# The last pair of token chunks takes w4 in seven block products for eight, and gives its output transposed

## The chip, the cores and the metric

One core of one Trainium2 chip runs the whole program. The metric is the device time of one execution in microseconds; of several executions the median is taken.

## The reference

Two layers, and each adds two parts to a residual stream `x` of 2048 tokens by 512 channels: a Fourier mixing by matrix products, and an MLP block. The second half of the MLP block, which the change is about, is a gelu between two matrices of 512 x 1376 and 1376 x 512.

```python
x1 = x + hs
h2 = _gelu(_layernorm(x1, axis=-1) @ w3) @ w4
return x1 + h2
...
x = A_x
x = x + _A_ref(_layernorm(x, axis=-1), A_dft_seq_re, A_dft_seq_im, A_dft_hid_re, A_dft_hid_im)
x = x + _B_ref(_layernorm(x, axis=-1), B_w1, B_w2, B_w3, B_w4)
x = x + _A_ref(_layernorm(x, axis=-1), A_dft_seq_re, A_dft_seq_im, A_dft_hid_re, A_dft_hid_im)
x = x + _B_ref(_layernorm(x, axis=-1), B_w1, B_w2, B_w3, B_w4)
```

## The kernel before

All numbers are fp32. A product of two fp32 blocks is made of three matmuls (`mm3`): each operand is split into a high part (a cast to fp32r on ScalarE, "ACT") and a low part (a subtraction on VectorE, "DVE"), and high x high, high x low and low x high are added up in PSUM. So every operand tile costs one ACT and one DVE instruction beside the matmuls that use it, and every block product of 128 x 128 by 128 x 512 costs three matmuls on TensorE ("PE").

The Fourier part streams the big matrices from HBM: a piece of 512 KB lands in one of four `raw` buffers (`issue_dma`, line 205), is split or summed into one of four `ring` slots by `stage_one` and `stage_two` (lines 220 to 241), and is used by the matmuls. Each layer goes over four chunks `c` of 512 tokens; for a chunk an x phase (`x_phase`) is followed by a y phase (`y_phase`). The x phase calls `hook(i)` at 16 steps, and what stands in the hook is put into the instruction streams there.

The MLP part (`by_pairs`) takes the tokens as two pairs of chunks, `c1` and `c2`. The hidden width is padded to 11 tiles of 128 channels (`NF`). A pair begins with the odd tile (w3e), and then goes over five steps `p`, of two hidden tiles each. In each step w3 is taken by seven products for eight (`prod`, a Strassen scheme with the sums of the inputs in `blk` and of the outputs in `u`, `v`, `x`, `y`), 42 matmuls of 512 columns. Its w4 products are plain ones: `w4_part` adds one hidden tile into four PSUM banks of 128 tokens by 512 channels, with the hidden tile as the stationary operand and w4 as the moving one: 12 matmuls for each tile and chunk. Those of `c1` stand between the steps, those of `c2` after them, and the results are added to `x` (`drain`) and stored.

There is one list of instructions for each engine, in the order in which the code is written; no scheduler moves them. All loads and stores are issued by SyncE ("SP") in that order too, so a load that waits for its buffer holds back every later one. Of the transfers in flight at most eight are allowed: each also waits for the one issued eight places earlier.

Of the kernel before, what the change touches and what calls it, by code (L numbers as in the profile page):

```python
# [8 lines left out]
F32 = mybir.dt.float32  # L9
F32R = mybir.dt.float32r  # L10
AF = mybir.ActivationFunctionType
ALU = mybir.AluOpType

P = 128
S, D, F = 2048, 512, 1376
# [4 lines left out]
CH = 512  # L20
NC = S // CH
TC = CH // P
KD = D // P
DH = D // 2
NF = -(-F // P)
B = 32
NB = P // B
LAG = 2
# [14 lines left out]
def spectral_mlp_kernel(ctx: ExitStack, tc: tile.TileContext, x, ws, hs, w1, w2, w34, out):  # L43
    nc = tc.nc
# [3 lines left out]
    dram = ctx.enter_context(tc.tile_pool(name="dram", bufs=1, space=bass.MemoryType.DRAM))  # L48
    ctx.enter_context(tc.manual_schedule())

    tmp = const.tile([P, 6, D], F32, name="tmp")
# [8 lines left out]

    w3d = [dram.tile([P, 2, 7, 2 * P], F32, name=f"w3d{i}") for i in range(NF // 2)]
    w3e = dram.tile([P, 2, CH], F32, name="w3e")
    w4d = [dram.tile([P, 2, CH], F32, name=f"w4d{i}") for i in range(NF)]


# [4 lines left out]
    AX, AY = 3 * 2 * DH, 4 * 2 * DH  # L70
    W12, XS = 2 * ZW, 2 * ZW + 8 * 2 * CH
    H3 = XS + NT * D
    SPARE = H3 + (LAG + 1) * 2 * CH
    RR = SPARE + 2 * D
    RNG = RR + 2 * KD * 2 * CH
    base = -(-nc.sbuf_base // 32) * 32
    EXT = RNG + RING * 4 * CH
    RAWS = EXT + 6 * D
    STG = RAWS + RAW * 2 * CH
    nc.alloc_sbuf_tensor("arena", [P, STG + 2 * CH], F32)  # L80

    def at(name, word, *shape, dtype=F32R):
        return nc.alloc_sbuf_tensor_at(name, [P, *shape], dtype, offset=base + 4 * word).ap()

    def both(name, word, *shape):
        return at(name, word, *shape), at(name + "f", word, *shape, dtype=F32)
# [7 lines left out]
    xs = [at(f"xs{i}", XS + i * 2 * D, 2, D, dtype=F32) for i in range(NP)]  # L94
# [8 lines left out]
    blk, blkf = {}, {}  # L103
# [4 lines left out]
    w3b, w3bf = zip(*(both(f"w3b{i}", RNG + 8 * CH + i * 28 * P, 2, 7, 2 * P) for i in range(2)))  # L108
    h4 = [at(f"h4{i}", RR + 8 * CH + i * 2 * CH, 2, CH) for i in range(4)]
# [7 lines left out]
    rest = [at(f"rest{i}", RAWS + i * D, D, dtype=F32) for i in range(8)]  # L117

    def xt(j):
        return xs[j // 2][:, j % 2]  # L120

    PA, PB, PC, PD = ([psum.tile([P, CH], F32, name=f"ps{i}{j}") for j in range(2)] for i in "abcd")
    acc4 = PC + PB
    mm4 = PD + PA
# [30 lines left out]
    for layer in range(LAYERS):  # L155
        for c in range(NC):
# [5 lines left out]
            for k in range(NP):  # L162
# [4 lines left out]
                p = piece(ws[c, k][:, 2:4])  # L167
# [26 lines left out]
    def rows(sb, d, j, n, load):  # L194
        v = d[j * P : (j + n) * P, :].rearrange("(t p) d -> p t d", p=P)
        nc.sync.dma_start(*((sb, v) if load else (v, sb)))
# [77 lines left out]
        return slots.pop(i)  # L274


    def mm3(o, lh, ll, rh, rl, first, last):
        nc.tensor.matmul(o, lh, rh, start=first, stop=False)  # L278
        nc.tensor.matmul(o, lh, rl, start=False, stop=False)  # L279
        nc.tensor.matmul(o, ll, rh, start=False, stop=last)  # L280

    def stats(srcs):

# [140 lines left out]
    def low(tf):  # L424
        nc.vector.tensor_tensor(tf[0][:, :, 1], tf[1][:, :, 1], tf[0][:, :, 0].bitcast(F32), op=ALU.subtract)
# [37 lines left out]
    def add(o, a, b, op=ALU.add):  # L463
        nc.vector.tensor_tensor(o, a, b, op=op)  # L464
# [123 lines left out]
    def turn_one(t, q, u):  # L588
        v = t.rearrange("p d (a q j) -> p d a q j", a=NB, q=TC)[:, :, :, q]
        nc.vector.transpose(v, blocks_of(u))  # L590

    def turn_out(t, to=None):

        if to is None:
            count["turn"] += 1
            to = zd[count["turn"] % 2]
        z = to.rearrange("(e i) t -> i e t", i=B)
        for b in range(NB):
            v = t[b * B : (b + 1) * B].rearrange("i d (a t) -> i (d a) t", a=NB)
            nc.sync.dma_start(z[:, :, b * P : (b + 1) * P], v)  # L600
# [35 lines left out]
    def split(dst, g, copy=nc.vector.tensor_copy):  # L636
        copy(dst[:, 0], g)  # L637
        split_low(dst, g)
# [74 lines left out]

        add(*(blkf[i][:, :, 1] for i in (o, a, b)), ALU.subtract)

    def prod(o, w, u, b):
        for d in range(2):
            v = slice(d * P, (d + 1) * P)
            mm3(o, w[:, 0, u, v], w[:, 1, u, v], blk[b][:, d, 0], blk[b][:, d, 1], d == 0, d == 1)

    def last_of(layer):
        return layer == LAYERS - 1
# [4 lines left out]
    def by_pairs(layer, zs, xin, dst):  # L727
# [78 lines left out]
        def w4_load():  # L806
            n = seq["n"]
            if n == n_pairs * len(order) or layer == 0 and n >= len(order) and n - used["n"] > 3:
                return
            src, i = order[n % len(order)], w4_slot(n)  # L810
            nc.sync.dma_start(w4r[i].bitcast(F32), w3e if src is None else w4d[src])
            seq["n"] += 1

        def w4_use():
            used["n"] += 1
            return w4r[w4_slot(used["n"] - 1)]
# [141 lines left out]
        def drain(c, acc):  # L958
            for q in range(TC):
                nc.vector.tensor_tensor(xt(c * TC + q), acc[q], xt(c * TC + q), op=ALU.add)  # L960
# [7 lines left out]
        def one():  # L968
            if bg:
                bg.pop(0)()  # L970
# [41 lines left out]

        for pair in range(n_pairs):
            c1, c2 = 2 * pair, 2 * pair + 1
            kept, next_too = bool(layer or pair), pair == n_pairs - 1 and not last_of(layer)
            hcs = [hc[:, f] for f in range(NF)]
            if next_too:
# [1 line left out]
                bg += early  # L1019
            if pair:  # L1020
                bg.insert(0, lows("t4"))
            sets = [rest[4:8], [tmp[:, i] for i in range(4)] if layer and pair else rest[4:8]]
            bk, acc1 = (acc4, mm4) if pair == 0 else (mm4, acc4)
            acc2 = [bk[(1 + i) % 4] for i in range(4)]
            if pair == 0:
# [132 lines left out]
                    rows(xs[j // 2], dst, j, 2, False)  # L1158
            split_later(2)
            split_later(3)  # L1160
            last = layer and pair == n_pairs - 1
            for k in range(NF - 2 if last else NF):
                w4_part(acc2, fs[k], h4[(2 + k) % 4])
                w4_load()
                if k:
                    split_later(k + 3)
                one()
                after_part(k + 2)
            if last:
                ss = [w4_use(), w4_use()]  # L1170
                for q in range(TC):
                    v = slice(q * P, (q + 1) * P)
                    for k, s in zip((NF - 2, NF - 1), ss):
                        h = h4[(2 + k) % 4]
                        mm3(acc2[q], h[:, 0, v], h[:, 1, v], s[:, 0], s[:, 1], False, k == NF - 1)
                    j = c2 * TC + q
                    nc.vector.tensor_tensor(xt(j), acc2[q], xt(j), op=ALU.add)
                    rows(xs[j // 2][:, j % 2 : j % 2 + 1], dst, j, 1, False)
            else:
                drain(c2, acc2)  # L1180
                for j in range(c2 * TC, c2 * TC + TC, 2):
                    rows(xs[j // 2], dst, j, 2, False)
                while bg:
                    one()


    w4_from = [(w34[NF - 1][:, 0], w3e)] + [(w34[f + LAG][:, 1], w4d[f]) for f in range(NF)]
# [2 lines left out]
    def w4_split(i):  # L1190
        for n in (i - 5, i - 4, i - 3):
            if 0 <= n <= NF:
                w, wf = w4_in[n % 4]
                if n == i - 5:
                    nc.vector.tensor_tensor(w[:, 1], wf[:, 1], w[:, 0].bitcast(F32), op=ALU.subtract)
                    nc.sync.dma_start(w4_from[n][1], w.bitcast(F32))
                elif n == i - 4:
                    nc.scalar.copy(w[:, 0], wf[:, 1])
                else:
                    nc.sync.dma_start(wf[:, 1], w4_from[n][0])  # L1200

    for layer in range(LAYERS):
        xin = x if layer == 0 else x2d
# [3 lines left out]
        for c in range(NC):  # L1207
# [82 lines left out]
            def hook(i):  # L1290
                k, odd = divmod(i, 2)
                if layer == 0 and c == 1:
                    if i == 1:
                        xp_sums(NP - 1)
                    if i == 2:
                        xp_highs(NP - 1, False)
                    if i == 3:
                        xp_lows(NP - 1, False)
                    w4_split(2 * NP + i)
                if c == 0:  # L1300
                    if layer:
                        for step, f in zip((0, 0, 1), (ay_sums, ay_highs, ay_lows)):
                            if i == step:
                                f(5)
                        for k, first, stages in (
                            (6, X6, xp_stages),
                            (7, X7, (xp_stats, xp_norm, ax_sums, ax_highs, ax_lows)),
                        ):
                            for step, f in zip((0, 1, 3, 4, 6), stages):
                                if i == first + step:  # L1310
                                    f(k)
                    return
                j = (c - 1) * TC
                if i == 4:
                    rows(X1, xin, j, 2, True)
                if i == 9:
                    rows(X1, x1d, j, 2, False)
                if i == 10:
                    rows(X1, xin, j + 2, 2, True)
                if c == NC - 1 and i in BACK:  # L1320
                    rows(xs[BACK[i] // 2], x1d, BACK[i], 2, True)
# [105 lines left out]
```

## Time and profile before

| | |
|---|---|
| times of 3 runs | 1442.24, 1442.72, 1443.43 us; median 1442.72 us |
| span of the profiled execution | 1440.5 us |
| PE busy | 1433.3 us, 6312 matmuls |
| DVE busy | 1127.9 us |
| ACT busy | 714.8 us |
| moved by DMA | 297.35 MB, mean 206 GB/s |

The span runs from the first to the last instruction of the profiled execution. A busy time is the time in which an engine has at least one instruction running; the matmuls overlap, so the busy time of PE is not the sum over them. For the profiled execution only the span is listed; its own time as the three runs are timed is not, so the median of the runs stands for it, 2.2 us above the span.

### The profile page before, as it was taken

What the parts mean: (1) busy time and instruction counts of PE and PEld (TensorE: products, weight loads), DVE (VectorE), ACT (ScalarE), POOL (GpSimd) and SP (SyncE); (2) the same over time, 40 slices, a digit from 0 to 9 for tenths busy, and PEclk for the clock granted to TensorE, in tenths of its full rate; (3) what the DMA queues carried; (4) which work ended last, traced back from release to release, by engine and by line L of the source; (5) the groups of instructions that cost most, each with busy time, mean ns of one, the idle gap of its engine ahead of it and who ended that gap; (6) DMA issues with size and microseconds to landing.
All of it is one profiled execution on the core that took longest, in us unless ns stands there. A gap on an engine that the chain in (4) does not pass through costs nothing.

```text
span 1440.5 us, 17253 instructions
## 1 busy us (share of the span) xinstructions
PE 1433.3 (99%) x6312; PEld 1181.6 (82%) x6312; DVE 1127.9 (78%) x1559; ACT 714.8 (50%) x954; POOL 82.2 (6%) x111
## 2 busy tenths in 40 slices
PE   9999999999999999999999999999999999999998
PEld 7888888888888888888888888888888888888887
DVE  7986997987969787666799979889798787656442
ACT  6663454455565644444555544545455574433231
POOL 2100000000002000000000000000000010000000
PEclk9999999999999999999999999999999999999999
DMA  7866655657655857944645565565666466578434
GB/s 258 268 205 204 205 185 197 203 179 258 206 175 130 289 199 239 364 159 154 239 142 189 190 199 196 168 228 173 231 216 225 141 178 252 199 246 322 161 127 158
DMA packets 117796, 297.35 MB, mean 206 GB/s; under 512 B 8784, under 2 KB 41552, under 8 KB 115152
## 3 DMA queue, kind: packets, MB, share of 16 engines
q1 hardware_dynamic: 117712, 296.26, 61.3%
q8 instruction: 49, 0.80, 0.2%
q14 instruction: 35, 0.29, 0.1%
HBM read 249.30 MB, written 46.92 MB: 206 GB/s over the span
## 4 chain that ended last, share of the span: by engine, by line
PE 95%; DVE 2%; ACT 1%; issue 1%; POOL 0%; DMA 0%; DVEq 0%; ACTq 0%; POOLq 0%
PE psd L278 10%; PE psd L280 10%; PE psd L279 10%; PE psa L278 8%; PE psa L280 8%; PE psa L279 8%; PE psc L280 7%; PE psc L279 7%; PE psc L278 7%; PE psb L278 7%; PE psb L279 7%; PE psb L280 7%; DVE ring L241 0%; DVE xs L960 0%; DVE ay L391 0%
## 5 line engine op out<-in xcount | busy, mean ns | idle before, releaser
L223 ACT CAST ring<-raw 128x1024 fp32r<-128x1024 f32 x127 | 132.9, 1052 | 88.3 <-PE psd L280 40.0
L241 DVE TENSOR_TENSOR ring<-raw,ring 128x1024 fp32r<-128x1024 f32 (+1 forms) x128 | 154.8, 1212 | 21.6 <-ACT ring L223 20.9
L279 PE MATMUL psd<-ring,rr 128*128 128x512 f32 x208 | 81.0, 389 | 0.0
L278 PE MATMUL psd<-ring,rr 128*128 128x512 f32 x208 | 81.0, 389 | 0.0
L280 PE MATMUL psd<-ring,rr 128*128 128x512 f32 x208 | 81.0, 389 | 0.0
L631 ACT ACTIVATE tmp<-rest 128x512 f32<-128x512 f32 x36 | 22.8, 632 | 95.7 <-DVE rest L464 95.4
L318 POOL TENSOR_TENSOR rs<-ve,mhalf 128x4 f32<-128x4 f32 x16 | 27.8, 1738 | 610.7 <-DVE nm L317 610.7
L230 ACT CAST ring<-ring0f 128x1024 fp32r<-128x1024 f32 x28 | 29.6, 1056 | 58.6 <-DVE ring0f L229 58.6
L634 DVE TENSOR_TENSOR h<-hc,h 128x512 fp32r<-128x512 f32 x41 | 27.9, 690 | 37.2 <-ACT h L637 37.2
L241 DVE TENSOR_TENSOR ring<-ring1f,ring 128x512 fp32r<-128x512 f32 (+1 forms) x56 | 53.3, 952 | 0.7 <-ACT ring L226 0.7
L297 POOL TENSOR_TENSOR rs<-ve,mhalf 128x2 f32<-128x2 f32 (+1 forms) x33 | 28.1, 853 | 413.5 <-DVE nb L296 413.5
L637 ACT CAST h<-hc 128x512 fp32r<-128x512 f32 x41 | 25.3, 620 | 51.1 <-PE psd L279 17.0
L279 PE MATMUL psb<-ring,ay 128*128 128x512 f32 x128 | 50.1, 391 | 0.0
L279 PE MATMUL psc<-ring,ay 128*128 128x512 f32 x128 | 49.9, 390 | 0.0
L280 PE MATMUL psc<-ring,ay 128*128 128x512 f32 x128 | 49.9, 390 | 0.0
L280 PE MATMUL psb<-ring,ay 128*128 128x512 f32 x128 | 49.8, 389 | 0.0
L278 PE MATMUL psc<-ring,ay 128*128 128x512 f32 x128 | 49.8, 389 | 0.0
L278 PE MATMUL psb<-ring,ay 128*128 128x512 f32 x128 | 49.8, 389 | 0.0
L279 PE MATMUL psa<-ring,ay 128*128 128x512 f32 x126 | 49.1, 390 | 0.0
L280 PE MATMUL psa<-ring,ay 128*128 128x512 f32 x126 | 49.1, 389 | 0.0
L278 PE MATMUL psa<-ring,ay 128*128 128x512 f32 x126 | 49.1, 389 | 0.0
L279 PE MATMUL psd<-ring,ay 128*128 128x512 f32 x126 | 49.1, 389 | 0.0
(440 smaller groups left out, 4419.2 us busy)
## 6 DMA issues: line engine op xcount, KB each, us to landing
raw<-in_ws SPq DMA_DIRECT2D x183, 512.0 KB, 5.0
w4r<-w4d SPq DMA_DIRECT2D x88, 512.0 KB, 4.2
raw<-in_hs SPq DMA_DIRECT2D x56, 512.0 KB, 3.7
w3b<-w3d SPq DMA_DIRECT2D x15, 1792.0 KB, 7.3
w3d<-w3b SPq DMA_DIRECT2D x5, 1792.0 KB, 6.9
x1d<-tmp SPq DMA_DIRECT2D x12, 512.0 KB, 6.3
xs<-x1d SPq DMA_DIRECT2D x12, 512.0 KB, 6.5
w4d<-w4in SPq DMA_DIRECT2D x11, 512.0 KB, 4.7
```

The source lines that it names most:

```text
L223: nc.scalar.copy(dest[:, a:b, 0], r[0][:, a:b])
L230: nc.scalar.copy(dest[:, :, 0], lo)
L241: nc.vector.tensor_tensor(lo[:, i], src[:, i], hi[:, i].bitcast(F32), op=ALU.subtract)
L278: nc.tensor.matmul(o, lh, rh, start=first, stop=False)
L279: nc.tensor.matmul(o, lh, rl, start=False, stop=False)
L280: nc.tensor.matmul(o, ll, rh, start=False, stop=last)
L297: nc.gpsimd.tensor_tensor(rs[:, :n], ve[:, :n], mhalf[:, 0, :n], op=ALU.pow)
L318: nc.gpsimd.tensor_tensor(rs, ve, mhalf[:, :, :2], op=ALU.pow)
L631: nc.scalar.activation(g_of, ps_of, AF.Gelu_apprx_tanh)
L634: nc.vector.tensor_tensor(dst[:, 1], g, dst[:, 0].bitcast(F32), op=ALU.subtract)
L637: copy(dst[:, 0], g)
```

## The change

The last pair of the second layer leaves the loop of `by_pairs` and gets a function of its own, `last_pair`. There the w3 steps run one behind the other, without w4 in between, and all 55 hidden tiles and sums are kept (`hs_`). Two hidden tiles by two chunks, and w4's two rows of tiles by two halves of 256 channels, then make a 2 x 2 block product, taken by the same seven products for eight: four of them in a first stretch over the five steps `k`, three in a second. w4 is the stationary operand now and the hidden tiles (512 tokens) are the moving one, so the output comes as channels by tokens. The odd tile (`h11`) is taken plainly. The residual is transposed on DVE (`turn_x`), written to HBM (`xtd`) and read back (`rt`). The upper half of the output is written transposed, and the host turns it back.

The sums of w4's blocks that the seven products need are made once, in the x phases of layer 0's chunks 2 and 3 and of layer 1's chunks 1, 2 and 3, one step `k` in each: a load at hook step 2, four sums on DVE and a cast on ACT at step 10, a subtraction on DVE and a store of 1 MB at step 11.

```diff
+    w4s = [dram.tile([P, 4, 2, 2 * P], F32, name=f"w4s{i}") for i in range(NF // 2)]
+    xtd = [dram.tile([D, CH], F32, name=f"xtd{i}") for i in range(2)]
...
         def w4_load():
             n = seq["n"]
             if n == n_pairs * len(order) or layer == 0 and n >= len(order) and n - used["n"] > 3:
+                return
+            if last_of(layer) and n > len(order):
                 return
...
+            if last_of(layer) and pair == n_pairs - 1:
+                last_pair(c1, c2, dst, w4_use)
+                continue
...
+    def last_pair(c1, c2, dst, w4_use):
...
+        w3c = [w3b[1], w3b[0], at("w3c", XS, 2, 7, 2 * P)]
+        w3c = [w3c[i] for i in (0, 1, 2, 0, 1)]
...
+        def load_1(k):
+            t = u1[k % 3].bitcast(F32)
+            for i in range(2):
+                nc.sync.dma_start(t[:, i], w4d[2 * k + i][:, :, : 2 * P])
+            nc.sync.dma_start(t[:, 2:4], w4s[k][:, 0:2])
...
+        def parts_of(of, k):
+            for f in (high_of, low_of):
+                for n in h_in_1 if of is hi_1 else h_in_2:
+                    f(of, k, n)
...
+        def product(o, w, hi, lo, first, last):
+            for i in range(2):
+                v = slice(i * P, (i + 1) * P)
+                mm3(o[i], w[:, 0, v], w[:, 1, v], hi, lo, first, last)
...
+        nc.sync.dma_start(w11.bitcast(F32), w4d[NF - 1])
+        load_1(0)
+        w3_bring(2)
+        for p in range(nk):
...
+            prod(b1, w, 4, "11")
+            act(u, b1)
+            prod(b6, w, 1, "t2")
+            add(v, u, b6)
+            then(0)
+            prod(b7, w, 2, "t3")
+            add(x, v, b7)
+            then(1)
+            prod(b5, w, 0, "t1")
+            add(y, x, b5)
+            gelu_to("22", y)
+            prod(b1, w, 5, "21", new=False)
+            gelu_to("11", b1)
+            then(2)
+            prod(b4, w, 6, "t4")
+            add(x, x, b4)
+            gelu_to("21", x)
+            then(3)
+            prod(b5, w, 3, "22", new=False)
+            add(v, v, b5)
+            gelu_to("t3", v)
+            if p < 2:
+                w3_bring(p + 3)
+            one()
+        load_1(1)
+        load_1(2)
+        parts_of(hi_1, 1)
+        t_sum(nk - 1, 0, 1, 2, 3)
...
+        for k in range(nk):
+            t = u1[k % 3]
+            for o, unit, n in ((p1, 0, "11"), (p6, 3, "t2"), (p5, 2, "t1"), (p2, 1, "21")):
+                if k == 0 and o is p2:
+                    product(p2, w11[:, :, : 2 * P], h11[0][:, 0], h11[0][:, 1], True, False)
+                product(o, t[:, unit], hi_1(k, n), hs_[k][n][0], k == 0 and o is not p2, k == nk - 1)
+            if k + 2 < nk:
+                parts_of(hi_1, k + 2)
+            else:
+                parts_of(hi_2, k + 2 - nk)
+            if k + 3 < nk:
+                load_1(k + 3)
+            load_2(k)
+            if k < 2:
+                nc.sync.dma_start(rt[k], xtd[k].rearrange("(d p) t -> p d t", p=P))
...
+        second(p4, 0, "t4", nk - 1, False)
+        for i in range(2):
+            add(v[:, i], v[:, i], p4[i])
+            store(v, c1, 1, i)
+        for i in range(2):
+            w = slice(i * P, (i + 1) * P)
+            t = u2[nk - 1][:, 2]
+            mm3(p3[i], t[:, 0, w], t[:, 1, w], hi_2(nk - 1, "22"), hs_[nk - 1]["22"][0], False, True)
+            add(x[:, i], x[:, i], p3[i])
+            store(x, c2, 0, i)
...
+        if i == 10:
+            a, b = (w4_raw[:, :, h * 2 * P : (h + 1) * 2 * P] for h in range(2))
+            s = w4_sumf[:, :, 1]
+            add(s[:, 0], b[:, 0], b[:, 1])
+            add(s[:, 1], s[:, 0], a[:, 0], ALU.subtract)
+            add(s[:, 2], a[:, 0], b[:, 0], ALU.subtract)
+            add(s[:, 3], a[:, 1], s[:, 1], ALU.subtract)
+            nc.scalar.copy(w4_sum[:, :, 0], s)
+        if i == 11:
+            nc.vector.tensor_tensor(
+                w4_sum[:, :, 1], w4_sumf[:, :, 1], w4_sum[:, :, 0].bitcast(F32), op=ALU.subtract
+            )
+            nc.sync.dma_start(w4s[k], w4_sum.bitcast(F32))
```

PE, in the last pair, between the w3 products of one step and of the next: before, the last matmuls of a plain w4 tile (stationary `h4`, moving `w4r`) are followed by w3's product with `t4` (`bt4`).

```order
L278 MATMUL psc1_241<-w4r2_211,h43_203 128x512
L279 MATMUL psc1_241<-w4r2_211,h43_203 128x512
L280 MATMUL psc1_241<-w4r2_211,h43_203 128x512
L278 MATMUL psb0_238<-w4r2_211,h43_203 128x512
L279 MATMUL psb0_238<-w4r2_211,h43_203 128x512
L280 MATMUL psb0_238<-w4r2_211,h43_203 128x512
L278 MATMUL psb1_239<-w4r2_211,h43_203 128x512
L279 MATMUL psb1_239<-w4r2_211,h43_203 128x512
L280 MATMUL psb1_239<-w4r2_211,h43_203 128x512
L278 MATMUL psa1_237<-bt4_194,w3b1_198 128x512
```

PE now, in the first stretch, at the change from step 0 to step 1: `hia` are the high parts of the hidden tiles, `hs` their low parts, `u1` the w4 blocks.

```order
L281 MATMUL psa0_243<-hs1_9387,u10_9481 128x512
L282 MATMUL psa0_243<-hia3_9459,u10_9481 128x512
L280 MATMUL psa1_244<-hia4_9460,u11_9482 128x512
L281 MATMUL psa1_244<-hs7_9399,u11_9482 128x512
L282 MATMUL psa1_244<-hia4_9460,u11_9482 128x512
L280 MATMUL psc0_247<-hia4_9460,u11_9482 128x512
L281 MATMUL psc0_247<-hs7_9399,u11_9482 128x512
L282 MATMUL psc0_247<-hia4_9460,u11_9482 128x512
```

The moving operand is still 512 columns wide, a hidden tile is used for two matmul groups instead of four, and over the whole program PE has 30 rows fewer.

DVE, in the x phase of layer 0's chunk 2, at hook steps 10 and 11 (before, then now; `ring` and `raw` are the stream's buffers, `ring1f` the sum of a slot):

```order
L241 TENSOR_TENSOR ring_170<-ring1f,ring_170 128x512
L241 TENSOR_TENSOR ring_172<-raw_176,ring_172 128x2x512
L241 TENSOR_TENSOR ring_174<-raw_177,ring_174 128x2x512
L225 TENSOR_TENSOR ring1f<-raw_178 128x512
L241 TENSOR_TENSOR ring_168<-raw_178,ring_168 128x2x512
```

```order
L243 TENSOR_TENSOR ring_177<-ring1f,ring_177 128x512
L243 TENSOR_TENSOR ring_179<-raw_183,ring_179 128x2x512
L466 TENSOR_TENSOR w4sumf<-w4raw 128x256
L466 TENSOR_TENSOR w4sumf<-w4sumf,w4raw 128x256
L466 TENSOR_TENSOR w4sumf<-w4raw 128x256
L466 TENSOR_TENSOR w4sumf<-w4raw,w4sumf 128x256
L243 TENSOR_TENSOR ring_181<-raw_184,ring_181 128x2x512
L1435 TENSOR_TENSOR w4sum<-w4sumf,w4sum 128x4x256
L227 TENSOR_TENSOR ring1f<-raw_185 128x512
```

Five instructions stand between those of the stream, and each place of the five has the same ones.

More of the change, by code (lines that the diff above doesn't have):

```diff
@@ L274, in stream, with mm3 @@
         return slots.pop(i)
[L277 to L280, printed above, removed]
+    def mm3(o, lh, ll, rh, rl, first, last, more=False):
+        nc.tensor.matmul(o, lh, rh, start=first, stop=False, skip_group_check=more)
+        nc.tensor.matmul(o, lh, rl, start=False, stop=False, skip_group_check=more)
+        nc.tensor.matmul(o, ll, rh, start=False, stop=last, skip_group_check=more)
     def stats(srcs):
@@ L714, in b_sum, with prod @@
         add(*(blkf[i][:, :, 1] for i in (o, a, b)), ALU.subtract)
-    def prod(o, w, u, b):
+    def prod(o, w, u, b, new=True):
         for d in range(2):
             v = slice(d * P, (d + 1) * P)
-            mm3(o, w[:, 0, u, v], w[:, 1, u, v], blk[b][:, d, 0], blk[b][:, d, 1], d == 0, d == 1)
+            mm3(o, w[:, 0, u, v], w[:, 1, u, v], blk[b][:, d, 0], blk[b][:, d, 1], new and d == 0, d == 1, not new)
     def last_of(layer):
@@ L1021, in by_pairs @@
                 bg.insert(0, lows("t4"))
-            sets = [rest[4:8], [tmp[:, i] for i in range(4)] if layer and pair else rest[4:8]]
+            sets = [rest[4:8], rest[4:8]]
             bk, acc1 = (acc4, mm4) if pair == 0 else (mm4, acc4)
@@ L1160, in by_pairs @@
             split_later(3)
-            last = layer and pair == n_pairs - 1
-            for k in range(NF - 2 if last else NF):
+            for k in range(NF):
                 w4_part(acc2, fs[k], h4[(2 + k) % 4])
@@ L1168, in by_pairs @@
                 after_part(k + 2)
[L1169 to L1178, printed above, removed]
-            else:
[L1180 to L1184, printed above, removed]
+            drain(c2, acc2)
@@ L1200, in w4_split, with w4_bring, w4_sums @@
                     nc.sync.dma_start(wf[:, 1], w4_from[n][0])
+    w4_raw = at("w4raw", STG, 2, CH, dtype=F32)
+    w4_sum, w4_sumf = both("w4sum", 5 * AY, 4, 2, 2 * P)
+    W4_AT = {(0, 2): 0, (0, 3): 1, (1, 1): 2, (1, 2): 3, (1, 3): 4}
+    def w4_bring(k):
+        nc.sync.dma_start(w4_raw, w34[2 * k + LAG : 2 * k + LAG + 2, :, 1].rearrange("f p w -> p f w"))
+    def w4_sums(k, i):
+        if i == 2:
+            w4_bring(k)
+        if i == 10:
[11 more added lines that the diff above has]
+            nc.sync.dma_start(w4s[k], w4_sum.bitcast(F32))
     for layer in range(LAYERS):
@@ L1312, in hook @@
                     return
+                if (layer, c) in W4_AT:
+                    w4_sums(W4_AT[layer, c], i)
                 j = (c - 1) * TC
@@ L1423 @@
     r = run_bass_kernel_spmd(nc, [arrays], core_ids=[0])
+    got, half = r.results[0]["out"], S // 2
     out = np.empty((S, D), a["A_x"].dtype)
-    out[at] = r.results[0]["out"]
+    out[at[:half]] = got[:half]
+    out[half:] = got[half:].reshape(D, half).T
     return out.reshape(_OUT)
```

122 lines of the change are left out of this document (added).

## The prediction

> **What bounds the kernel now.** The page comes first: how busy the engines are, and by what the chain that ended last is made.
>
> ```profile
> span 1440.5 us, 17253 instructions
> PE 1433.3 (99%) x6312; PEld 1181.6 (82%) x6312; DVE 1127.9 (78%) x1559; ACT 714.8 (50%) x954; POOL 82.2 (6%) x111
> PE 95%; DVE 2%; ACT 1%; issue 1%; POOL 0%; DMA 0%; DVEq 0%; ACTq 0%; POOLq 0%
> ```
>
> PE is busy for 99% of the span, and 95% of the chain is its matmuls. Next the waits of PE, over the whole program:
>
> ```profile
> PE psd L132 <- POOL mhalf L55: 1.4, 1, 1.4
> PE psc L279 <- DVE ring L241: 0.7, 1, 0.7
> PE psc L410 <- ACT rr L1242: 0.2, 1, 0.2
> ```
>
> PE waits 2.3 us in all, and never in the last pair. So whatever takes matmuls away shows in full, as long as the other engines and the loads keep up; and there is no wait left whose going could bring more. Last, what a matmul costs at its pace. These are the first and the last one of the last pair in the timeline (start, duration, engine, line):
>
> ```profile
> 1322.50 0.39 PE L278 MATMUL psd<-b,w4r 128*128 128x512 f32 x1
> ...
> 1435.15 0.39 PE L280 MATMUL psd<-w4r,h 128*128 128x512 f32 x1
> ```
>
> The code issues 498 matmuls here: 24 for w3e, 5 x 42 for w3, 22 x 12 for w4. From first to last there are 497 steps in 112.65 us, 0.2267 us each. The duration of 0.39 us overlaps the next ones, and is not the price.
>
> **The change part by part: matmuls.** All matmuls of the pair stay 512 columns wide. The plain w4 products were 2 chunks x 11 tiles x 12 = 264. Now the five steps take 7 products x 6 matmuls = 42 each, 210, and the odd tile 4 x 6 = 24: 234. That is 30 fewer, at 0.2267 us: **-6.80 us**. The roles of the operands are swapped, but both kinds of product lie in the same 112.65 us at one pace, so I take the pace as kept.
>
> The Trainium skill, page "TensorE: Matmul & The Clock Gate", section "Back-to-back issue gap", gives N / 2.4 + 2.5 ns, 215.8 ns for 512 columns; by it the sum would be -6.47 us. The trace has 226.7 ns, and the trace decides.
>
> **DVE and ACT in the last pair.** What the added instructions cost, from the groups of the lines view from 1270 us on (mean ns after the bar) and, for the transpose, from the view of its line (min/median/max):
>
> ```profile
> L464 DVE TENSOR_TENSOR rest<-rest,psd 128x512 f32<-128x512 f32 x11 | 7.6, 687 | 10.8 <-PE psd L280 10.8
> L634 DVE TENSOR_TENSOR h<-hc,h 128x512 fp32r<-128x512 f32 x22 | 15.0, 691 | 25.4 <-ACT h L637 25.4
> L464 DVE TENSOR_TENSOR bt2f<-b22f,bt1f 128x1024 f32<-128x1024 f32 x1 | 1.2, 1226 | 0.0
> L637 ACT CAST h<-hc 128x512 fp32r<-128x512 f32 x22 | 13.7, 621 | 33.9 <-PE psd L279 14.7 <-PE psc L279 7.7 <-PE psb L279 5.8
> L631 ACT ACTIVATE tmp<-rest 128x512 f32<-128x512 f32 x9 | 5.7, 632 | 32.7 <-DVE rest L464 32.7
> L590 DVE STREAM_TRANSPOSE scr<-rest x8: 668/708/712, 466.9 to 1180.3; 128x512 f32<-128x512 f32 x8
> ```
>
> A w3 step now lasts 42 x 0.2267 = 9.5 us on PE. DVE has 5 sums out of PSUM and from p = 1 on 4 sums of hidden tiles, 9 x 0.69 = 6.2 us; with two transposes 7.6 us; in the worst step, p = 3, three lows more: 8.3 us. ACT has 5 x 0.63 = 3.2 us, with four casts 5.6 us. It fits.
>
> The first stretch takes 24 x 0.2267 = 5.4 us a step, against 4 lows (2.8 us) and 4 casts (2.5 us). At its start the parts of step 1 follow the last sum (0.69), a gelu (0.63), a cast (0.62) and a low (0.69): the first pair is there after 2.6 us, and PE, with the odd tile's 6 matmuls in step 0, wants it after 30 x 0.2267 = 6.8 us. Those of step 2 stand behind the rest of them and four sums, and come until some 10.3 us; PE wants them at 12.2 us. In the second stretch a step is 4.1 us against three lows, 2.1 us. I cost all this at nothing; its cover is PE, and where it fails it costs the lateness itself.
>
> **The loads of the last pair.** w3's last three blocks now come within 43 us instead of being spread over twice that, and w4 comes in pieces. What the queue gives is read from the DMA view, for 1300 to 1330 us (runs of 2 KB and more) and 1240 to 1280 us (many runs of 512 bytes), and for 1322 to 1376 us, of which the second row is the landing time of one block of w3:
>
> ```profile
> DMA packets 2894, 10.01 MB, mean 334 GB/s; under 512 B 272, under 2 KB 272, under 8 KB 2759
> q1 hardware_dynamic: 2890, 9.97, 88.7%
> ...
> DMA packets 5283, 8.51 MB, mean 213 GB/s; under 512 B 240, under 2 KB 4336, under 8 KB 5026
> q1 hardware_dynamic: 5282, 8.49, 69.0%
> ...
> DMA packets 2053, 10.44 MB, mean 193 GB/s; under 512 B 195, under 2 KB 195, under 8 KB 1675
> w3b<-w3d SPq DMA_DIRECT2D x3, 1792.0 KB, 7.2
> ```
>
> The queue holds 334 GB/s over 30 us; with runs of 512 bytes 213 / 0.69 = 309 GB/s when it is busy. Now count from the pair's first matmul; I set the start of the flow at 5 us, since w4's first blocks wait for the second product of w3e (24 x 0.2267 = 5.4 us) and w3's block of p = 2 stands behind them on SP. Until PE wants that block at 5.4 + 2 x 9.5 = 24.4 us, 4.46 MB must come (output rows 1.05, `w11` 0.52, w4 1.05, w3 1.84): a rate of 4.46 / 19.4 = 230 GB/s. Until p = 4 at 43.6 us it is 9.2 MB (two blocks of w3 and a transposed residual more): 238 GB/s. In the first stretch the w4 blocks of k = 3 and k = 4, between them `u2` and `rt`, are 3.67 MB, free to be loaded from the end of step 0 on and wanted 16.3 us later: with 1.4 us of latency (my estimate, from the 2.0 us that 256 KB took to land, below, less their 0.7 at 334 GB/s) 246 GB/s. Runs of 1 KB, which these loads have, the trace does not show; they lie between the two rows, and I take the lower, 309. All three demands are below it, so this costs nothing; at 200 GB/s it would cost 11 us (rival C). Bounds: 0 to 11, the value 0 nearest to both rows.
>
> **The sums beside the x products.** At each of the five places DVE gets four sums of 256 columns. From 1226 ns for 1024 columns and 687 for 512 I estimate 0.42 us each, 1.7 us, and 1.22 us for the low; ACT one cast, about 1.05 us; SP two issues. DVE at the first place now, in the timeline and in the table of stages:
>
> ```profile
> 230.17 1.23 DVE L241 TENSOR_TENSOR ring<-raw,ring 128x1024 fp32r<-128x1024 f32 x1 [1.49 <-ACT ring L223]
> 233.13 0.69 DVE L225 TENSOR_TENSOR ring1f<-raw 128x512 f32<-128x512 f32 x1 [1.73 <-PE psa L280]
> ...
> 237.89 1.37 DVE L464 TENSOR_TENSOR tmp<-psd,tmp 128x512 f32<-128x512 f32 x2 [2.33 <-PE psd L280]
> ...
> 226.00:241.00 15.00, 15.00 (x68) 12.43 (x67) 8.56 (x10) 5.46 (x6) 0.03 (x1) 1.00 0.68 232
> ```
>
> DVE is idle for 15.00 - 8.56 = 6.4 us of these 15, in gaps that PE ends: it waits for PE to free a slot. 2.9 us go into that. On SP the store of the sums waits for the low, and behind it the next `raw` loads wait. They wait there anyway:
>
> ```profile
> SPq L205 <- DVE ring L241: 341.1, 121, 8.4
> ```
>
> The 1.5 MB of a place are some 5 us of the queue at 309 GB/s, in a phase that moves 232 GB/s. The ring holds up to four slots of 2.7 us (12 matmuls) each, so a few us of lateness do not reach PE. Zero, with bounds of 0 and 2 us over all five; a gain is excluded, since PE does not wait there.
>
> **The end.** Now four stores of 256 KB follow each other at 6 x 0.2267 = 1.36 us:
>
> ```profile
> 1434.22 0.69 DVE L1177 TENSOR_TENSOR xs<-psa,xs 128x512 f32<-128x512 f32 x1 [0.67 <-PE psa L280]
> 1435.58 0.69 DVE L1177 TENSOR_TENSOR xs<-psd,xs 128x512 f32<-128x512 f32 x1 [0.67 <-PE psd L280]
> ...
> out<-xs SPq DMA_DIRECT2D x4, 256.0 KB, 2.0
> ```
>
> In the changed kernel a result tile is finished every 3 matmuls, 0.68 us, and its sum takes 0.69: the last sum ends 0.05 us later than now after the last matmul. 256 KB each 0.69 us are 380 GB/s, at 334 each store takes 0.10 us more than its turn: about 0.3 us over the last four. Bounds: 0, and 1.6 at 213 GB/s. I take +0.3.
>
> **Sum.** -6.80 + 0.3 + 0 + 0 = -6.5 us: a span of 1434.0 for 1440.5. The three runs have their median at 1442.72, 2.2 us above the span; I take that as unchanged: **1436.2 us**.
>
> **The rivals.** *A, the forecast:* all cover holds, 1436.2; from 1435.2 (no cost at the end, and the 0.7 us by which runs of a kernel differ) to 1438. *B, a part is given back:* a late block of w3 or w4 in the last pair, 1 to 4 us, about 1438.7. For it: the demands of 230 to 246 GB/s are not far under 309, and a window of the pair moves only 193 GB/s now; against it: there SP waits for PE to free buffers, not the queue for bandwidth. *C, slower: the loads bound the last pair.* At 200 GB/s the block of p = 2 comes at 5 + 4.46 / 0.2 = 27.3 us, 2.9 late, that of p = 4 at 51 us, 7.4 late in all, and the w4 blocks of k = 4 3.5 us late: 11 us, so 1442.7 - 6.5 + 11 = 1447.2. It decides where lateness eats 6.5 us: 12.9 MB in 60 us, 215 GB/s. For it: the page's mean of 206 GB/s, and pieces of 1 KB and 512 bytes; against it: both rows above. *D, no change: the x phases pay.* If each place held up PE for 1.3 us, all 6.5 us would be gone, 1442.7. For it: SP stands still for the store, and the window moves 232 GB/s already; against it: the gaps on DVE and the ring's lead.
>
> What a long wait would do to the clock, the end of the trace hints at (window, PE and the other engines busy, granted clock third from the end):
>
> ```profile
> 1435.00:1440.50 5.50, 0.54 (x3) 0.12 (x1) 0.69 (x1) 0.00 (x0) 0.00 (x0) 0.92 0.28 105
> ```
>
> The Trainium skill, the same page, section "HAM oscillation — how this bites in real kernels", says that a gap of more than about 3.4 us halves the clock until PE has been busy again as long; in C that would add some 1.7 us for each wait of that length. The trace agrees as far as the clock falls to 0.92 in these idle us; C's price stands without it.
>
> **Numbers.** A 0.78, B 0.09, C 0.08, D 0.05. A measurement here tells 0.2% from no change, 2.9 us, so faster means under 1439.8: A and most of B, 0.86; same is D and the rest of B, 0.06; slower is C, 0.08. The range holds A and most of B: 1435.2 to 1439.5.
>
> **What would show it.** Right: 30 matmuls fewer on PE; the last pair 468 matmuls in about 106 us; PE's waits still some 2 us in all; the last store landing 2 to 2.3 us after its issue. Wrong: PE waiting for a DMA into `w3c`, `w3b` or `u1` (B, C), for `ring` in the five x phases (D), or for `hs` and `hia` (my count of DVE or ACT); or a pace other than 0.2267 us with the operands swapped.

## The result, and the profile after

| | before | after |
|---|---|---|
| median of 4 runs each | 1442.55 us (1442.24 to 1443.43) | 1435.47 us (1435.16 to 1435.71) |
| ratio | | 0.9951, 95% interval 0.9937 to 0.9965 |
| span of the profiled execution | 1440.5 us | 1433.3 us |

The change is faster by 7.1 us; 1436.2 had been forecast. The host's turning of the upper half of the output lies outside this time, and no run measures it. The page of the changed kernel, first the span, the busy times and what the chain is made of:

```profile
span 1433.3 us, 17344 instructions
PE 1426.0 (99%) x6282; PEld 1175.0 (82%) x6282; DVE 1168.3 (82%) x1629; ACT 728.3 (51%) x976; POOL 82.2 (6%) x111
PE 90%; DVE 6%; ACT 1%; DMA 1%; issue 1%; POOL 0%; SPq 0%; DVEq 0%; POOLq 0%; ACTq 0%
```

PE has 6282 matmuls for 6312, the 30 fewer of the forecast, and it is still busy for 99%. DVE has 70 instructions and 40.4 us more, ACT 22 and 13.5 us. The chain has 90% of PE for 95% before, but PE is not short of work for that: the waits say what it lacked (us in total, times, longest):

```profile
PE psd L134 <- POOL mhalf L55: 1.4, 1, 1.4
PE psc L281 <- DVE ring L243: 0.7, 1, 0.7
PE psb L412 <- ACT rr L1480: 0.6, 1, 0.6
PE psa L282 <- DVE rg L636: 0.6, 1, 0.6
PE psc L412 <- ACT rr L1480: 0.2, 1, 0.2
```

That is 3.5 us, all of it ahead of the last pair: from 1322 us to the end the view is empty. The first and the last matmul of the last pair, in the timeline:

```profile
1323.41 0.39 PE L280 MATMUL psd<-b,w4r 128*128 128x512 f32 x1
...
1429.26 0.39 PE L282 MATMUL psd<-hib,u 128*128 128x512 f32 x1
```

Now the difference of the two executions can be cut into three. The pair begins 0.91 us later (1323.41 for 1322.50). From its first to its last matmul it takes 105.85 us for 112.65: 467 steps of 0.2267 us, so the 30 matmuls are worth 6.80 us to the second digit. And from the last matmul's start to the end of the span it is 4.04 us for 5.35, 1.31 less. 0.91 - 6.80 - 1.31 = -7.2, which is the difference of the spans. The first and the last part had not been forecast so; the experiments take them up.

### The profile page after: what moved, and what is told of

Its sections match the earlier page's. It is cut to its first block, busy times and chain, and to the rows that moved or that the text cites. A ratio compares the mean times of both kernels' runs of the same rounds, so it can differ in the third digit from the quotient of the medians.

```text
span 1433.3 us, 17344 instructions
## 1 busy us (share of the span) xinstructions
PE 1426.0 (99%) x6282; PEld 1175.0 (82%) x6282; DVE 1168.3 (82%) x1629; ACT 728.3 (51%) x976; POOL 82.2 (6%) x111
## 4 chain that ended last, share of the span: by engine, by line
PE 90%; DVE 6%; ACT 1%; DMA 1%; issue 1%; POOL 0%; SPq 0%; DVEq 0%; POOLq 0%; ACTq 0%
PE psd L280 9%; PE psd L282 9%; PE psd L281 9%; PE psc L281 7%; PE psc L282 7%; PE psc L280 7%; PE psa L280 7%; PE psb L281 7%; PE psa L282 7%; PE psb L280 7%; PE psb L282 7%; PE psa L281 7%; DVE ring L243 1%; DMA zt1f<-zd 1%; DMA raw<-in_ws 0%
## 5 line engine op out<-in xcount | busy, mean ns | idle before, releaser
L243 DVE TENSOR_TENSOR ring<-raw,ring 128x1024 fp32r<-128x1024 f32 (+1 forms) x128 | 154.6, 1211 | 14.3 <-ACT ring L225 13.5
L633 ACT ACTIVATE tmp<-rest 128x512 f32<-128x512 f32 x30 | 19.0, 632 | 73.0 <-DVE rest L466 72.7
L280 PE MATMUL psd<-ring,ay 128*128 128x512 f32 x126 | 49.0, 389 | 0.0
L281 PE MATMUL psd<-ring,ay 128*128 128x512 f32 x126 | 49.0, 389 | 0.0
L282 PE MATMUL psd<-ring,ay 128*128 128x512 f32 x126 | 49.0, 389 | 0.0
```

What stands on the lines that cost most here:

```text
L243: nc.vector.tensor_tensor(lo[:, i], src[:, i], hi[:, i].bitcast(F32), op=ALU.subtract)
L280: nc.tensor.matmul(o, lh, rh, start=first, stop=False, skip_group_check=more)
L281: nc.tensor.matmul(o, lh, rl, start=False, stop=False, skip_group_check=more)
L282: nc.tensor.matmul(o, ll, rh, start=False, stop=last, skip_group_check=more)
L633: nc.scalar.activation(g_of, ps_of, AF.Gelu_apprx_tanh)
```

## The experiments

The theory (A: the matmuls are what counts, all other work is covered) stood against B and C (the loads come late, or bind), D (the sums cost what the products save) and one more that the result brought: that the end of the program, not the products, gave part of the gain. Where ends or pairs are compared, the numbers are the first and last matmul in the timeline of each profiled execution.

**The sums alone.** The kernel before gets only the making of w4's sums in the x phases:

```diff
+    w4s = [dram.tile([P, 4, 2, 2 * P], F32, name=f"w4s{i}") for i in range(NF // 2)]
...
+                if (layer, c) in W4_AT:
+                    w4_sums(W4_AT[layer, c], i)
```

> The kernel before, plus only the sums of w4's blocks in the five x phases, whose results nobody reads. Theory (the sums lie in gaps of DVE, ACT and SP and cost PE nothing): the time of before within 0.3 us, about 1442.6, PE's waits 2 to 3 us as before. Rival (the sums cost what the changed kernel's last pair started later, 0.9 us in its trace at 1323.41 for 1322.50): 1443.4, with a new wait of PE in the layer's MLP part or an x phase. Rival D of the prediction (each place holds up PE by 1.3 us): 1449.

Measured: 1442.33 us (11 runs, 1441.54 to 1443.40) for 1442.77 of the kernel before (21 runs), ratio 0.9997 [0.9988, 1.0006], a cost between -1.7 and +0.9 us. D asked for 6.5 us more and is refuted. How the cover works is seen in the changed kernel, in DVE's timeline at the first of the five places and in the table of stages:

```profile
228.71 0.42 DVE L466 TENSOR_TENSOR w4sumf<-w4raw 128x256 f32<-128x256 f32 x1
229.16 0.42 DVE L466 TENSOR_TENSOR w4sumf<-w4sumf,w4raw 128x256 f32<-128x256 f32 x1
...
231.43 1.22 DVE L1435 TENSOR_TENSOR w4sum<-w4sumf,w4sum 128x1024 fp32r<-128x1024 f32 x1
233.24 0.69 DVE L227 TENSOR_TENSOR ring1f<-raw 128x512 f32<-128x512 f32 x1 [0.59 <-PE psa L282]
```

```profile
226.00:241.00 15.00, 15.00 (x68) 12.42 (x67) 11.13 (x16) 6.52 (x7) 0.14 (x1) 1.00 0.89 309
```

A sum of 256 columns takes the 0.42 us that had been estimated, and DVE's busy time in these 15 us goes from 8.56 to 11.13. Ahead of the sum `ring1f` there was a gap of 1.73 us; now it is 0.59. The gap of 1.49 us ahead of the instruction at 230.17 us, which a cast on ACT had ended, is gone too. So the added work lies in the two gaps, and `ring1f` starts 0.11 us later, as does the instruction ahead of the sums (226.00 us for 225.89). PE is busy for all 15 us in both.

**The scheme without the sums.** The other side: the changed kernel doesn't make the sums, and loads as many bytes of other blocks in their place.

```diff
-            nc.sync.dma_start(t[:, 2:4], w4s[k][:, 0:2])
+            nc.sync.dma_start(t[:, 2:4].rearrange("p u h w -> p (u h w)"), w4d[2 * k].rearrange("p h w -> p (h w)"))
...
-                if (layer, c) in W4_AT:
-                    w4_sums(W4_AT[layer, c], i)
```

> The changed kernel without the sums of w4's blocks; the last pair loads parts of w4 itself in their place, so its products are of other blocks. Theory (the sums cost nothing): the changed kernel's 1435.5 within 0.3 us. Rival (the sums cost 0.9 us): 1434.6, and the last pair starts at 1322.5 again.

Measured: 1435.62 us (1434.44 to 1435.71), ratio 0.9947 [0.9935, 0.9960]; the changed kernel itself had 1435.47. Nothing comes back, so both sides agree: the sums cost nothing that these runs can tell from zero. Nor is there a sign that they delay the last pair: with the sums alone it begins at 1322.79 us, and without them at 1323.58, in one execution each.

**30 matmuls more and 30 fewer.** If PE alone sets the length of the pair, its price must follow the count in both directions, and in the direction of fewer until something else binds. First one product of the first stretch is taken twice in each of the five steps:

```diff
-                product(o, t[:, unit], hi_1(k, n), hs_[k][n][0], k == 0 and o is not p2, k == nk - 1)
+                product(o, t[:, unit], hi_1(k, n), hs_[k][n][0], k == 0 and o is not p2, k == nk - 1 and o is not p2)
+                if o is p2:
+                    product(o, t[:, unit], hi_1(k, n), hs_[k][n][0], False, k == nk - 1)
```

> The changed kernel with one of the seven products taken twice in every step of the first stretch, 30 matmuls of the same operands more; that product counts double in the output. All else stays. Theory (the gain is the number of matmuls at 0.2267 us, all else hidden): 1435.5 + 6.8 = 1442.3, with the tail as in the changed kernel. Rival (part of the gain is from the new shape of the pair, fewer w4 loads or plain order): it stays clearly under 1442.

Then the same product is left out, and the odd tile's closes its sum:

```diff
-                    product(p2, w11[:, :, : 2 * P], h11[0][:, 0], h11[0][:, 1], True, False)
-                product(o, t[:, unit], hi_1(k, n), hs_[k][n][0], k == 0 and o is not p2, k == nk - 1)
+                    product(p2, w11[:, :, : 2 * P], h11[0][:, 0], h11[0][:, 1], True, True)
+                if o is not p2:
+                    product(o, t[:, unit], hi_1(k, n), hs_[k][n][0], k == 0, k == nk - 1)
```

> The changed kernel without one of the seven products (21 by the second w4 block) in the five steps of the first stretch: 30 matmuls fewer, that term is missing in the output. The steps of the first stretch shrink from 5.44 to 4.08 us, while its casts, lows and loads stay. Theory (PE bounds, with room left): 1435.5 - 6.8 = 1428.7. Rival (DVE, ACT or the loads are just under PE): by the prediction's counts the w4 blocks of k = 3 and 4, 3.67 MB, are now wanted 12.2 us after the end of step 0 instead of 16.3, 340 GB/s with the latency, and the parts of a step take 2.8 us on DVE of 4.08: 1 to 4 us of waits of PE for u1, so 1430 to 1433.

Measured: 1442.40 us (ratio 0.9998 [0.9989, 1.0006]) and 1428.54 (0.9902 [0.9887, 0.9917]); against 1435.47 that is +6.93 and -6.93, 0.231 us a matmul. By the ratios, which compare with the kernel before in the same session, it is +6.8 and -7.1. The first and last matmul of the pair in the timelines of the two, in this order:

```profile
1324.10 0.39 PE L280 MATMUL psd<-b,w4r 128*128 128x512 f32 x1
...
1436.75 0.39 PE L282 MATMUL psd<-hib,u 128*128 128x512 f32 x1
```

```profile
1323.16 0.39 PE L280 MATMUL psd<-b,w4r 128*128 128x512 f32 x1
...
1422.21 0.39 PE L282 MATMUL psd<-hib,u 128*128 128x512 f32 x1
```

The pairs last 112.65 and 99.05 us, 6.80 to either side of 105.85, and neither shows a wait of PE in the pair. The first of these kernels has as many matmuls as the kernel before and the changed kernel's end: its median is within 0.4 us of 1442.77, with an interval of -1.6 to +0.9 us. So in the medians it is the 30 matmuls that make the difference, and all the rest together is too small to be told from zero; parts of it that cancel each other are not excluded.

**More loads: every w4 load twice, and three times.** How near do the loads come to binding?

```diff
+            for i in range(2):
+                nc.sync.dma_start(t[:, i], w4d[2 * k + i][:, :, : 2 * P])
+            nc.sync.dma_start(t[:, 2:4], w4s[k][:, 0:2])
...
+            nc.sync.dma_start(t[:, 0], w4d[2 * k + 1][:, :, 2 * P :])
+            nc.sync.dma_start(t[:, 1:3], w4s[k][:, 2:4])
```

> The changed kernel with every load of w4 blocks in the last pair issued twice, the second one bringing the same bytes. Theory (the loads lie under PE with a margin that a rate of 385 GB/s, seen in the changed kernel's first stretch, allows): until the blocks of k = 4 are there the queue must now move some 6.6 MB from the end of step 0 on, 17.1 us and the latency of 1.4, against 16.3 to 17.7 us in which PE wants them: 1 to 2 us late there, some more in the second stretch; 1 to 5 us in all, 1436.5 to 1440.5, with PE waiting for a DMA into u. Rival (the loads have far more room, since they wait for buffers and not for the queue): 1435.5. Rival C of the prediction (the queue gives about 200 GB/s for runs of 1 KB): 33 us for these bytes, over 1450.

> The changed kernel with every load of w4 blocks in the last pair issued three times. Theory (a rate of about 385 GB/s bounds it): 9.5 MB until the blocks of k = 4, 25 us against 17, and waits for each block of the second stretch too: 20 to 35 us, 1455 to 1470. Rival (buffers, not the queue, hold the loads): under 1445.

Measured: 1461.73 us (1.0133 [1.0118, 1.0149]) and 1496.97 (1.0373 [1.0356, 1.0390]). Both lie far above what the theory gave, and the first in the range that was named for C, over 1450. SP's own waits from 1320 us on, with the loads twice, show that it is not C's reason:

```profile
SPq L1224 <- DMA u<-w4d: 24.6, 5, 7.0
SPq L1217 <- DMA u<-w4d: 16.3, 6, 5.8
```

Lines 1217 and 1224 are second loads, as are 1218 and 1225 with 6.0 and 3.4 us more. The second load of a tile goes to the place of the first, so it waits until that has landed, and every later load stands behind it on SP: 50.3 us of standing still. The queue meanwhile is not full: its share is 0.77 from 1376 to 1404 us and 0.75 from 1404 to 1432, at 242 and 244 GB/s. So it is in the main a chain of latencies, not a lack of bandwidth, and this pair of runs doesn't say how much the queue could bear. It had to be asked in another way.

**More bytes into unused memory.** Behind each group of w4 loads, but for the first, 512 KB (and then 1 MB, by `range(2)`) are read into buffers that nobody uses, three in turn:

```diff
+        def more_bytes(k):
+            for _ in range(1):
+                nc.sync.dma_start(pads[pad_n[0] % 3], w4d[k])
+                pad_n[0] += 1
...
+            if k:
+                more_bytes(k)
...
+            more_bytes(k)
```

> The changed kernel with 512 KB more read from HBM behind each group of w4 loads from k = 1 of the first stretch on and of the second, into memory that nothing else uses, so that no load of w4 has to wait for another to the same place: nine loads, 4.7 MB more in the 28 us of the first stretch and what follows. Theory (the queue gives some 385 GB/s, and the loads of the changed kernel have room): no wait of PE for u, 1435.3 within 0.4 us. Rival (the margin is under 1 us, as the run with each load issued twice could mean): PE waits 2 to 7 us for u, 1437 to 1442, which is what a rate of 250 GB/s would give.

> The same with 1 MB behind each group, 9.4 MB more. Theory (385 GB/s): at the edge, 0 to 3 us of waits for the blocks of k = 4, 1435.3 to 1438.5. At 310 GB/s: 8 us, 1443.5; at 250 GB/s: 22 us, 1457.

Measured: 1435.88 us (0.9950 [0.9933, 0.9966]) with 512 KB, 1437.42 (0.9962 [0.9947, 0.9977]) with 1 MB. The first lies 0.2 us above the theory's range (1435.3 within 0.4), but its trace has no wait of PE in the last pair; the second is within the theory's range. The first stretch, 28 us, in the table of stages (last three columns: granted clock, DMA share, GB/s) of the changed kernel, with 512 KB and with 1 MB:

```profile
1376.00:1404.00 28.00, 28.00 (x125) 23.21 (x124) 19.93 (x32) 16.11 (x29) 0.00 (x0) 1.00 0.81 281
```

```profile
1376.00:1404.00 28.00, 28.00 (x125) 23.22 (x124) 19.94 (x32) 15.96 (x28) 0.00 (x0) 1.00 0.89 310
```

```profile
1376.00:1404.00 28.00, 27.25 (x120) 21.95 (x119) 18.68 (x30) 15.38 (x28) 0.00 (x0) 1.00 0.97 358
```

and PE's waits in the last pair with 1 MB:

```profile
PE psa L280 <- DMA u<-w4s: 0.4, 1, 0.4
PE psc L280 <- DMA u<-w4s: 0.4, 1, 0.4
PE psa L280 <- DMA u<-w4d: 0.4, 1, 0.4
```

At 310 GB/s PE stays busy for all 28 us. At 358 GB/s, where the queue is full for 97% of the time, PE loses 0.75 us in the window, and the pair lasts 107.88 us, 2.0 more, of which the three waits are 1.2. So the change has a margin of somewhere between 512 KB and 1 MB a group, and its loads bind at a supply far above the 215 GB/s at which C had to decide. With 1 MB the three buffers come round so soon that SP also stands still for 20.4 us until an earlier block has landed in one of them, with the loads of w4 behind. The upper end of the margin is therefore not the queue's alone, though the queue was busy for 97% of the window all the same.

**The same two kernels once more.** The pair's start and the end of the span had moved by +0.91 and -1.31 us, of which one execution each can't say whether they belong to the kernel. Both kernels are run unchanged, one profiled execution each.

> The kernel before, unchanged, once more with a profile: from the last matmul's start to the end of the span it had 5.35 us and its last store landed after 3.2 us, while the kernel with the sums alone has 4.06 us with the same code at the end. Theory (one late store in one execution): about 4.05 us now, the last pair starting between 1322.5 and 1323.5. Rival (before's end is longer by itself): 5.3 us again.

> The changed kernel, unchanged, once more with a profile. Theory (the 0.9 us by which its last pair started later is the difference of two executions): a start anywhere from 1322.5 to 1324, the last pair 105.85 us from its first to its last matmul, 4.05 us from there to the end. Rival (the change delays what lies ahead of the pair): a start at 1323.4 within 0.2 us.

Measured: 1443.72 us with the pair beginning at 1323.60, and 1435.05 with 1323.02. So the start differs from execution to execution: with 1322.50 and 1323.60 before, 1323.41 and 1323.02 after, the kernels overlap. Over all the traces, the nine kernels and executions with `last_pair` begin it between 1322.82 and 1324.10 us, the three without it at 1322.50, 1322.79 and 1323.60; a later start by half a microsecond with the change is not excluded. The small waits for `rg` and `rr` ahead of the pair are there in one execution and absent or shorter in the next. The end does not vary so: it is 5.35 us again before and 4.03 after. The landing time of the last store (issue to landing, min/median/max), first before, then before again (three stores), then after (the last two):

```profile
DMA to landing us min/median/max: 3.2/3.2/3.2
```

```profile
DMA to landing us min/median/max: 2.0/2.0/3.2
```

```profile
DMA to landing us min/median/max: 2.0/2.0/2.1
```

The last sum ends 1.1 us after the last matmul's start in both kernels; the late landing is the difference. My first idea, that one execution before happened to have a late store, fell with the second execution. What lies beside it is in the DMA view of before, for 1438.1 to 1439.1 us (packets, MB, share):

```profile
q14 instruction: 1, 0.01, 1.9%
q1 hardware_dynamic: 1, 0.00, 0.1%
```

Narrower windows place them: the packet of the instruction queue comes at 1438.12 us and takes 0.31, and the packet of the store, one of under 512 bytes, comes at 1438.42, as the other ends and 0.4 us behind the store's packet before it. The store, issued at 1436.30 us, counts as landed at 1439.5, another 1.1 us on. Before again shows the same two rows from 1439.2 to 1440.2 us. The end of the kernel with the sums alone, whose code at the end is that of before but whose instructions are more in number, has no such packet, has the last packet of its store at 1438.2 us, lands it in 2.0 us (0.4 us after that packet) and ends 4.06 us after its last matmul's start. So where the instruction packet comes with the last store, the end was later by 1.3 us, in two executions of two. No run moved that packet and nothing else, so that it holds up the store is argued, not shown; and its 0.31 us would account for a part of the 1.2 us only, since more than half of the lateness lies between the store's last packet and its landing.

## Why the prediction was right, point by point

**The matmuls** (-6.80) are shown: the pair is 6.80 us shorter in the profiled execution, and 30 matmuls more or fewer moved the median by 6.93 to either side. The pace with w4 as the stationary operand is the same 0.2267 us. The rate that the Trainium skill gives in "TensorE: Matmul & The Clock Gate", section "Back-to-back issue gap" (by it -6.47), stands there for an isolated matmul; for this stream the measurement decides for 226.7 ns, which every pair without a wait shows, at a granted clock of 1.00.

**DVE and ACT in the last pair** (0) held: PE waits for no hidden tile there, in the changed kernel nor with 30 matmuls fewer, where DVE and ACT had less time. **The sums beside the x products** (0) held in both directions, though of the 6.4 us of gaps that the prediction lays to PE alone, the waits for casts of ACT were 2.4. **The loads** (0) held, with the margin that the added bytes found. The demand of the first stretch was counted too low: by the sizes of the loads (1024 KB each for the blocks of k = 3 and k = 4, 768 for `u2`, 1024 for `rt`) it is 3.93 MB and not 3.67, 264 GB/s by the prediction's own latency of 1.4 us (2.0 less 256 KB at 334 GB/s would be 1.2); still under 309. And only the halves of w4's tiles come in runs of 1 KB: from 1391.4 to 1404 us such packets are 1238 of 2739 and carry 26% of the bytes. For this mixture the rate that I took, 309 GB/s, was low; for runs of 1 KB alone no run shows one. The queue moves this much in the slices of 0.7 us from 1376 to 1404 us:

```profile
GB/s 279 281 119 269 269 257 174 31 12 0 0 0 35 348 377 309 189 130 215 288 329 328 401 398 392 401 386 391 376 405 367 404 386 392 379 377 391 392 380 380
```

It is 367 to 405 GB/s over the last 18 slices of the 40. **The end** (+0.3, bounds 0 and 1.6) is the term that was mis-sized, by sign too: -1.31 in the profiled execution, outside its bounds. It failed twice. The backlog of the four stores did not arise: they landed in 2.0 to 2.1 us at a turn of 0.69, 380 GB/s, for which the queue has room. And the row from which I took the old end, a median of 2.0 us over four stores, hid that the last of them took 3.2. With -6.80 - 1.31 the sum would have been 1432.4 for the span; 1433.3 was measured, since the pair began 0.91 us later in that execution. The forecast of the median, 1436.2, lies 0.7 above the result: 0.3 of that is this term, and the rest is no more than what the medians of the kernel before differ by themselves (1442.55, 1442.77, 1442.87 and 1443.21 in four comparisons). Nor does the 1.31 show in the medians: with as many matmuls, the kernel with 30 more is 0.4 us from the kernel before, in an interval that would just admit it. So the matmuls' term came out by its mechanism; that the whole came so near owes something to luck, since in the profiled execution the two shifts that were not foreseen, +0.91 and -1.31, had opposite signs.

**PE's waits** were to stay at some 2 us, and are 3.5, so this sign failed; the two that came, for `rr` (0.6) and `rg` (0.6), lie ahead of the pair in code that is as before, and run unchanged again, the changed kernel has 2.4 in all and the kernel before 3.0, with a wait of 0.7 for `rg`.

**The rivals.** B's late block did not come: no wait of PE in the last pair. C's threshold of 215 GB/s was far below what the queue gives; the mean of 206 GB/s on the page, which spoke for C, is what the program asks for, and no bound. D is refuted by the sums alone.

## What to carry to other kernels

PE was busy for 99% here, and the engines and the queue that took over the work had idle time in those very stretches. There the matmuls removed were worth their count times the measured step, and the sums, casts and loads that took their place cost nothing that the runs could tell. What a queue can give is read where it is pressed, not from its mean: here 206 GB/s on the page and up to 405 in a slice. And to ask how much load a stage bears, add bytes that nobody waits for, with buffers enough that the added loads don't wait for each other; a second load to the same place measures a chain of latencies.

## What the runs showed of the hardware that had not been expected

A long wait halves the clock, as the prediction had it of rival C, and it stays halved for microseconds after the wait. With the loads twice PE waited 10.3 us for a block of w4; the stages (granted clock third from the end) and the timeline of the matmuls behind it:

```profile
1400.50:1404.00 3.50, 0.76 (x4) 0.29 (x2) 0.00 (x0) 0.00 (x0) 0.00 (x0) 0.93 0.89 246
1404.00:1408.00 4.00, 0.00 (x0) 0.00 (x0) 0.00 (x0) 0.00 (x0) 0.00 (x0) 0.50 1.05 389
```

```profile
1411.51 0.76 PE L280 MATMUL psa<-hia,u 128*128 128x512 f32 x1 [10.26 <-DMA u<-w4d]
1412.08 0.63 PE L281 MATMUL psa<-hs,u 128*128 128x512 f32 x1
1412.50 0.63 PE L282 MATMUL psa<-hia,u 128*128 128x512 f32 x1
```

The clock falls to 0.50 in the wait, and the matmuls behind it start 0.42 us apart for 0.2267. It is 0.50 for all of 1411.5 to 1420.5 us, with one more wait of 1.7 us in between, and 1.00 from 1420.6 on. The Trainium skill, page "TensorE: Matmul & The Clock Gate", section "HAM oscillation — how this bites in real kernels", puts the limit for idle stretches at some 3.4 us; the trace agrees for 10.3 us, and the waits of 0.4 us with 1 MB of added loads left the clock at 1.00. But a shorter one was enough with the loads three times, where PE waited 2.23 us; the stages before and after the wait's end, and the first matmuls behind it:

```profile
1403.50:1406.80 3.30, 1.40 (x6) 0.79 (x5) 1.90 (x3) 2.48 (x5) 0.00 (x0) 1.00 0.67 221
1406.90:1410.20 3.30, 2.90 (x6) 1.82 (x6) 2.99 (x5) 1.78 (x4) 0.00 (x0) 0.50 0.79 216
```

```profile
1407.14 0.77 PE L280 MATMUL psa<-hia,u 128*128 128x512 f32 x1 [2.23 <-ACT hib L1239]
1407.70 0.63 PE L281 MATMUL psa<-hs,u 128*128 128x512 f32 x1
```

There the measurement decides: the clock was 1.00 up to 0.3 us before that wait's end and 0.50 behind it, so a wait under 3.4 us can already cost it. The other surprise is the last store of the kernel before, which lands 1.2 us late beside a packet of the instruction queue, as told above; its cause stays open.
